# Chunk attention and a leaky two-layer product on one core: a build-time order that lets a load on Pool wait for the landing of the eighth preceding one, with 14 instead of 16 pieces by seven products

## The chip, the core and the metric

The kernel runs on one core of a Trainium2 chip. The core has a matrix engine (PE), a vector engine (DVE), a scalar engine (ACT), Pool (GpSimd) and SP, which here only issues transfers. Each engine works through its own list of instructions in order and waits on semaphores for the others. The metric is the time of one execution on the device in microseconds. A profiled execution gives the trace that the views are made from; its span runs from the first to the last instruction of the program.

## The reference

Inputs are q, k and v of shape (8 batches, 8 heads, 576, 64) and the weights w_in (512 x 2048) and w_out (2048 x 512), all float32.

```python
# attention inside chunks of 64 positions, nc = 9 chunks
scores = (1 / np.sqrt(D)) * np.matmul(q_c, k_c.transpose(0, 1, 2, 4, 3))
scores = scores - np.max(scores, axis=-1, keepdims=True)
attn = np.exp(scores)
attn = attn / (np.sum(attn, axis=-1, keepdims=True) + 1e-09)
out = np.matmul(attn, v_c)
...
# x: (4608 tokens, 512), heads side by side
h = x @ w_in
g = np.maximum(0.01 * h, h)
return (g @ w_out).astype(np.float32)
```

## The kernel before

**Attention by groups.** The 4608 tokens are 36 groups of 128 (two chunks, all eight heads). For a group `u`: its q and k are loaded by Pool's queue and cast to fp16 (`q_in`, `k_in`, eight buffers each, `NIN`); transposed; multiplied to scores (`Sp`, PE, L412); row maxima are taken and subtracted (`mx`, `sh`, DVE); ACT takes the exponential (`ex`); DVE sums and inverts (`z`, `ze`, `zi`); the result is normalised (`en`, on DVE, from group 24 on Pool); transposed again (`et`); multiplied by v (`xp`, PE, L477) and copied by ACT into the ring `xT`, where the second stage reads it. From group 9 on the transposes are DMA transposes issued by SP (`QT`, `KT`, `et`), and Pool copies the transposed q into the two zero-padded halves of a `QZ` buffer (L405, two copies per group, three buffers). The eight batches of v go into two buffers `VB`; batch b + 2 is loaded, in two halves, when the last `xp` that reads batch b has run.

**Two layers by blocks.** The tokens are also cut into 14 blocks, from block 7 on of 512 tokens. The first layer (w_in, then the leaky ReLU on ACT into `gT`) of a block runs beside the second layer of the block before. A block's first layer has four quarters. From block 8 on a plain quarter is four pieces of eight matmuls of 256 columns (`hT`, L165, 32 matmuls), each evicted by one ACT operation. A quarter can also be formed by seven products of half size in place of eight (`first_fast`, L763): 28 matmuls of 256 columns (`hA`, `hB`, `hC`, L297), three ACT copies to `tmp`, three DVE additions (L220), four leaky ReLUs on ACT. It needs four sums of weights (`VF`, formed once) and, per block, four differences of the inputs (`XF`, `x_form`, L257, on DVE). `FAST` says how many quarters of a block are formed so. The second layer of blocks 7 to 13 is always done by seven products (`second_fast`, L813), with sums of `gT` formed on DVE (`g_form`, L308).

**What sets the order.** Up to the middle of block 2 the order is written out by hand, loads included. After that a planner that runs while the program is built sets it. Each unit of work is a `Step` with an engine, an assumed duration, the steps it comes after, a key and a latency until others may use its result; `run()` (L574) repeatedly takes, over all engines, the step that can begin first (among those within 0.03 us on one engine the one with the smallest key), advances that engine's clock and emits the step's instructions. The plan moves nothing at run time: it decides in which order instructions stand in each engine's list. PSUM banks and `tmp` buffers are taken and given back by steps, so the plan also decides who shares a buffer.

In the plan a load was two steps: `load` on Pool (0.86 us, or 1.7 in two parts), then `arrive` on a separate timeline "dma" (2.05 us each, one after another, latency 2.5). Transposes on SP were given a latency of 10 us.

In the built program every DMA that Pool issues signals one of eight semaphores in turn. From the ninth on, a load waits at the head of Pool's list for the semaphore of the eighth preceding one. That wait stands in the program before as well as in the changed one.

Of the kernel before, what the change touches and what calls it, by code (L numbers as in the profile page):

```python
# [16 lines left out]
def kernel(  # L17
# [11 lines left out]
    B, H, S, D = q.shape  # L29
# [10 lines left out]
    NIN = 8  # L40
    UD = 9
    G = 2 * CH
# [5 lines left out]
    RING = 1536  # L48
    HB, HM = NFC // 2, d_model // 2
    NTMP = 7  # L50
    FAST = {10: 4, 11: 4, 12: 4, 13: 4}
    POOL_N, POOL_X = 24, 20

    sbp = ctx.enter_context(tc.tile_pool(name="k_sb", bufs=1))
# [519 lines left out]
    def run():  # L574
        now = {e: 0.0 for e in LAT}
        now["pool"] = 10.0
        left = {id(s): len(s.after) for s in steps}
        users: dict[int, list[Step]] = {}
        for s in steps:
            for x in s.after:  # L580
                users.setdefault(id(x), []).append(s)
        can = {e: [] for e in LAT}
        for s in steps:
            if not s.after:
                can[s.eng].append(s)
        INF = float("inf")

        def begin(s):
            t = max([now[s.eng], s.at] + [x.end + (x.lat if x.eng != s.eng or x.lat > 1 else LAG[s.eng]) for x in s.after])
            for pool in {h.pool for h in s.take}:  # L590
                n = sum(h.pool == pool for h in s.take)
                slots = sorted(y[0] for y in free[pool])
                if len(slots) < n + s.spare:
                    return INF
                t = max(t, slots[n - 1])
            return t

        order = []
        n = 0
        while True:  # L600
            best = None
            for e in LAT:
                if not can[e]:
                    continue
                at = [(begin(s), s) for s in can[e]]
                t0 = min(x[0] for x in at)
                if t0 == INF:
                    continue
                t, s = min((x for x in at if x[0] <= t0 + 0.03), key=lambda x: x[1].key)
# [24 lines left out]
    LAG = {"pe": 0.0, "act": 0.1, "dve": 0.1, "pool": 0.0, "sp": 0.0, "dma": 0.0}  # L634
    Step.spare = 0
    Step.name = ""

    def add(name, *a, spare=0, **k):
# [6 lines left out]
    get = done.get  # L645
# [6 lines left out]
    def group(u):  # L652
        at = max(0.0, BEGIN + (u - 5) * PACE)
        k = u / 4
        dve, act = 10 + k, 10 + k
        for i in range(2):
            if u >= UD + 4:
                add(("load", u, i), "pool", 0.86 if (u * G) // S == (u * G + G - 1) // S else 1.7, lambda u=u, i=i: load_half(u, i),
                    [get(("t", u - NIN, i)) or get(("pe_t", u - NIN, i)), get(("arrive", u - 4, i))], key=5 + u / 100, lat=0.5)
                add(("arrive", u, i), "dma", 2.05, lambda: None, [get(("load", u, i))], key=u, lat=2.5)  # L660
            elif u > 5:
                add(("arrive", u, i), "dma", 0.9, lambda: None, [], key=-9, at=2.2 + 1.8 * (u - 6) + 0.9 * i, lat=2.0)
        if 5 < u < UD:
            for i in range(2):
                h = Hold("bank")
                add(("pe_t", u, i), "pe", 0.23, lambda u=u, i=i, h=h: (stage_tq, stage_tk)[i](u, h.slot), [get(("arrive", u, i))],
                    key=-3, take=[h], spare=1)
                if i == 0:
                    for s in range(2):
                        add(("p", u, s), "dve", 0.42, lambda u=u, s=s: stage_q(u, s), [get(("pe_t", u, 0)), get(("s", u - NQZ))],  # L670
                            key=dve, give=[h] if s else [])
                else:
                    add(("k", u), "act", 0.5, lambda u=u: stage_k(u), [get(("pe_t", u, 1)), get(("s", u - 4))], key=act, give=[h])
        elif u >= UD:
            for i in range(2):
                add(("t", u, i), "sp", 1.28, lambda u=u, i=i: stage_t(u, i),
                    [get(("arrive", u, i)), get(("p", u - 4, 1)), get(("s", u - 4))], key=u, lat=10.0)
            for s in range(2):
                add(("p", u, s), "pool", 0.67, lambda u=u, s=s: stage_p(u, s), [get(("t", u, 0)), get(("s", u - NQZ))], key=u / 100)
        if u >= 5:  # L680
            h = Hold("bank")
            need = [get(("p", u, 0)), get(("p", u, 1)), get(("k", u)) or get(("t", u, 1))]
            add(("s", u), "pe", 0.24, lambda u=u, h=h: stage_s(u, h.slot), need, key=-2, take=[h], at=at)
            add(("m", u), "dve", 0.61, lambda u=u: stage_m(u), [get(("s", u)), get(("b", u - 2))], key=dve - 6)
            add(("b", u), "dve", 0.61, lambda u=u: stage_b(u), [get(("m", u)), get(("x", u - 2))], key=dve - 6, give=[h])
            add(("x", u), "act", 0.52, lambda u=u: stage_x(u), [get(("b", u)), get(("n", u - 2))], key=act - 4)
            add(("z", u), "dve", 1.15, lambda u=u: stage_z(u), [get(("x", u)), get(("n", u - 2))], key=dve - 4)
            add(("n", u), "pool" if u >= POOL_N else "dve", 1.0 if u >= POOL_N else 0.61, lambda u=u: stage_n(u),
                [get(("z", u)), get(("d", u - 3)) or get(("e", u - 3))], key=-1 if u >= POOL_N else dve - 4)
        if u < UD:  # L690
            h = Hold("bank")
            add(("e", u), "pe", 0.23, lambda u=u, h=h: stage_e(u, h.slot), [get(("n", u))], key=-2, take=[h])
            add(("d2", u), "dve", 0.34, lambda u=u: stage_c(u), [get(("e", u)), get(("v", u - 4))], key=dve - 3, give=[h])
        else:
            add(("d", u), "sp", 1.28, lambda u=u: stage_d(u), [get(("n", u)), get(("v", u - 4))], key=u, lat=10.0)
# [117 lines left out]
    def second_fast(j, k0):  # L813
        key = ("o", j)
        g = lambda f, e: G_OF[j, f, e]
        f0 = add(("sf", j, 0), "dve", 1.14, lambda: g_form(j, 0), g(0, 1) + g(1, 1) + [get(("m2", j - 1, 5, p)) for p in range(2)], key=6 + k0)
        f1 = add(("sf", j, 1), "dve", 1.14, lambda: g_form(j, 1), [f0] + g(0, 0) + [get(("m2", j - 1, 6, p)) for p in range(2)], key=6 + k0)
        f2 = add(("sf", j, 2), "dve", 1.14, lambda: g_form(j, 2), [f0] + g(0, 0), key=7 + k0)
# [56 lines left out]
        f3 = add(("sf", j, 3), "dve", 1.14, lambda: g_form(j, 3), [f1] + p2, key=6.5 + k0)  # L875
# [60 lines left out]
    for j in range(4, len(BLOCKS)):  # L936
# [10 lines left out]
        if fast:  # L947
            x = [y for y in x_of(j, 0, 512)]
            for i in range(4):
                add(("xf", j, i), "pool" if j >= POOL_X else "dve", 1.0 if j >= POOL_X else 0.35, lambda j=j, i=i: x_form(j, i),  # L950
                    x + ([get(("xf", j, {1: 0, 3: 1}[i]))] if i in (1, 3) else [])
                    + [get(("f", jj, ii, {0: 5, 1: 6, 2: 7, 3: 4}[i])) for jj, ii in fast_n if jj == j - 1],
                    key=5.8 + place)
# [46 lines left out]
```

## Time and profile before

| | us |
|---|---|
| median of three runs | 288.58 |
| lowest, highest | 287.51, 289.36 |
| the profiled execution's own time | 289.68 |
| span in its trace | 287.9 |
| mean granted clock of PE (share of full) | 0.988 |

What Pool's loads take from issue to landing, and SP's transposes, stands in the page's list of DMA issues (size, median us to landing):

```profile
q_in<-in_q_dram POOLq DMA_DIRECT2D x31, 128.0 KB, 7.1
k_in<-in_k_dram POOLq DMA_DIRECT2D x31, 128.0 KB, 7.5
...
QT<-q_in SPq DMA_TRANSPOSE x27, 6.2
KT<-k_in SPq DMA_TRANSPOSE x27, 5.9
et<-en SPq DMA_TRANSPOSE x27, 5.4
```

Rows of the other views are read like this. In groups of instructions: line, engine, operation, tile written, tile read, shapes, count, then busy us, mean ns of one, and the idle time of the engine just before them with what ended it. In the timeline: start, duration, instruction, and in brackets the idle time before it. Who ended an idle time is inferred from semaphores; where the engine named had long been done, another did. In the slices each digit is a fortieth of the span in tenths.

### The profile page before, as it was taken

The page shows a single profiled execution, that of the slowest core. Times are in us where ns is not written, and L with a number is a line of the kernel's source. Part 1 is how long each engine was busy: PE and PEld are TensorE (multiplying, and loading weights), DVE is VectorE, ACT ScalarE, POOL GpSimd, SP SyncE. Part 2 cuts the span into 40 slices and gives each one's busy share as a digit, 9 for nine tenths or more (in the row PEclk, how much of TensorE's full clock was granted, in tenths as well). Part 3 has the DMA queues.
Part 4 walks back from the last instruction along what each step waited for, and adds up shares of the span by engine and source line. Part 5 has one row for each costly group of instructions (what it writes and reads, how often), then busy time and mean ns, then how long its engine had stood idle before and what let it go on. Part 6 is the DMA issues. An engine that isn't in the chain of part 4 may idle for free.

```text
span 287.9 us, 7650 instructions
## 1 busy us (share of the span) xinstructions
PE 270.9 (94%) x3124; PEld 232.1 (81%) x3124; DVE 212.2 (74%) x364; ACT 176.1 (61%) x319; POOL 143.6 (50%) x178
## 2 busy tenths in 40 slices
PE   4989999994999999999999999988998999999995
PEld 4979846863686899999898988877797898988884
DVE  6988415993598569886966499988988994685472
ACT  6357723751464773737665449972699689578721
POOL 8857557937498256952985287674641111000000
PEclk9999999998699999999999999999999999999999
DMA  9999999999999999999999999997952101300223
GB/s 131 164 191 193 205 158 198 160 144 150 155 151 156 155 175 143 168 136 243 144 124 149 193 181 148 93 194 147 154 139 77 34 3 36 148 2 0 87 98 109
DMA packets 165794, 39.16 MB, mean 136 GB/s; under 512 B 156800, under 2 KB 161408, under 8 KB 165760
## 3 DMA queue, kind: packets, MB, share of 16 engines
q0 software_dynamic: 114336, 18.09, 94.8%
q1 hardware_dynamic: 50384, 20.33, 39.0%
q8 instruction: 24, 0.39, 0.6%
q10 hardware_dynamic: 1040, 0.26, 0.4%
q14 instruction: 10, 0.08, 0.1%
HBM read 36.70 MB, written 9.44 MB: 160 GB/s over the span
## 4 chain that ended last, share of the span: by engine, by line
PE 73%; DVE 14%; ACT 4%; issue 3%; POOL 3%; DMA 2%; DVEq 0%; ACTq 0%; POOLq 0%
PE hT L165 22%; PE oA L342 13%; PE oP L190 10%; PE hA L297 7%; PE oC L342 6%; PE hC L297 3%; PE oB L342 3%; PE Sp L412 2%; PE xp L477 2%; DVE tmp L220 2%; PE hB L297 2%; DMA k_f<-in_k_dram 2%; DVE gT L217 2%; DVE z L437 2%; DVE mx L421 2%
## 5 line engine op out<-in xcount | busy, mean ns | idle before, releaser
L165 PE MATMUL hT<-xT,w_inT 128*128 128x128 f16 (+1 forms) x960 | 79.3, 239 | 0.2 <-issue 0.2
L165 PEld LDWEIGHTS <-w_inT 128*128 128x128 f16 x960 | 68.0, 99 | 6.9 <-issue 0.9
L175 ACT ACTIVATE gT<-hT 128x512 f16<-128x512 f32 x80 | 47.3, 595 | 35.4 <-PE hT L165 34.9
L342 PEld LDWEIGHTS <-gT 128*128 128x128 f16 x560 | 54.1, 98 | 7.4 <-issue 1.3
L405 POOL COPY QZ<-QT 64x512 f16<-64x512 f16 x54 | 39.5, 732 | 16.1 <-DMA QT<-q_in 13.8
L421 DVE TENSOR_REDUCE mx<-Sp 128x8 f32<-128x512 f32 x36 | 24.5, 681 | 12.8 <-PE Sp L412 12.6
L175 ACT ACTIVATE gT<-tmp 128x512 f16<-128x512 f32 x48 | 29.7, 632 | 5.3 <-DVE tmp L220 5.3
L437 DVE TENSOR_REDUCE z<-ex 128x8 f32<-128x512 f16 x36 | 24.4, 679 | 11.3 <-ACT ex L431 11.2
L178 ACT ACTIVATE tmp<-hA 128x512 f32<-128x512 f32 x48 | 27.6, 598 | 7.9 <-PE hA L297 7.9
L190 PE MATMUL oP<-w_outT,gT 128*128 128x512 f16 x128 | 31.6, 387 | 0.0
L220 DVE TENSOR_TENSOR tmp<-hC,tmp 128x512 f32<-128x512 f32 x32 | 21.7, 681 | 11.3 <-ACT tmp L178 7.2
L489 ACT ACTIVATE xT<-xp 128x512 f16<-128x512 f32 x36 | 21.3, 594 | 14.0 <-PE xp L477 13.8
L431 ACT ACTIVATE ex<-sh 128x512 f16<-128x512 f32 x36 | 22.7, 630 | 10.8 <-DVE sh L425 10.1
L342 PE MATMUL oA<-WF,gT 128*128 128x256 f16 x224 | 27.9, 272 | 1.0 <-ACT tmp L178 1.0
L297 PEld LDWEIGHTS <-VF 128*128 128x128 f16 x256 | 24.6, 98 | 4.0 <-DVE XF L262 0.7
L447 POOL TENSOR_TENSOR en<-ex,zi 128x512 f16<-128x512 f16 x12 | 12.5, 1042 | 30.1 <-DVE zi L441 23.7
L912 POOL DMA_DIRECT2D VB<-in_v_dram x12 | 13.9, 1158 | 25.0 <-PE xp L477 25.0
L425 DVE TENSOR_TENSOR sh<-Sp,mx 128x512 f32<-128x512 f32 x36 | 24.5, 681 | 0.5
L342 PEld LDWEIGHTS <-S 128*128 128x128 f16 x224 | 20.9, 98 | 4.9 <-DVE S L220 2.2
L905 POOL DMA_DIRECT2D k_in<-in_k_dram x26 | 22.1, 853 | 4.1 <-PE hT L165 3.7
L905 POOL DMA_DIRECT2D q_in<-in_q_dram x26 | 22.1, 854 | 3.5 <-PE tpe L455 2.9
L178 ACT ACTIVATE tmp<-oA 128x512 f32<-128x512 f32 (+1 forms) x24 | 13.0, 540 | 15.7 <-PE oA L342 15.7
(71 smaller groups left out, 453.9 us busy)
## 6 DMA issues: line engine op xcount, KB each, us to landing
out_dram<-osb SPq DMA_DIRECT2D x12, 512.0 KB, 3.6
VB<-in_v_dram POOLq DMA_DIRECT2D x16, 288.0 KB, 7.3
q_in<-in_q_dram POOLq DMA_DIRECT2D x31, 128.0 KB, 7.1
k_in<-in_k_dram POOLq DMA_DIRECT2D x31, 128.0 KB, 7.5
out_dram<-osb SPq DMA_DIRECT2D x10, 256.0 KB, 5.5
w_inT<-in_moe_w_in_dram POOLq DMA_DIRECT2D x8, 256.0 KB, 8.8
w_outT<-in_moe_w_out_dram POOLq DMA_DIRECT2D x4, 512.0 KB, 10.3
q_in<-in_q_dram POOLq DMA_DIRECT2D x8, 64.0 KB, 9.4
```

The costliest lines, as they stand in the source:

```text
L165: nc.tensor.matmul(out=hT[:, i, :], lhsT=w_inT[:, t, fc * 128:(fc + 1) * 128], rhs=xT[:, t, r0 % RING:r0 % RING + tb], start=(t == 0), sto ...
L175: nc.scalar.activation(out=to, in_=of, func=AFT.Prelu, bias=0.0, scale=1.0, alpha=0.01)
L178: nc.scalar.activation(out=to, in_=of, func=AFT.Copy, bias=0.0, scale=1.0)
L190: nc.tensor.matmul(out=OP[j, ti], lhsT=gT(j)[:, fc, ti * 128:(ti + 1) * 128], rhs=w_outT[:, fc, :], start=(fc == 0), stop=(fc == NFC - 1),)
L220: nc.vector.tensor_tensor(out=to, in0=a, in1=b, op=ALU.add)
L297: nc.tensor.matmul(out=PA[key][:, c, :], lhsT=w[:, t, fc * 128:(fc + 1) * 128], rhs=x[:, t, :], start=(m in OPENS and c == 0 and t == 0), ...
L342: nc.tensor.matmul(out=to, lhsT=lhs[:, fc, p * 128:(p + 1) * 128], rhs=rhs[:, fc, :], start=(fresh and fc == 0), stop=(fc == HB - 1), skip ...
L405: nc.gpsimd.tensor_copy(out=QZ[u % NQZ][part, :, :, s, :], in_=QT[u][part])
L421: nc.vector.tensor_reduce(out=MX[u], in_=SP[u], axis=AXL.X, op=ALU.max)
L425: nc.vector.tensor_tensor(out=SH[u], in0=SP.pop(u), in1=MX.pop(u).unsqueeze(2).to_broadcast((128, 8, CH)), op=ALU.subtract)
L437: nc.vector.tensor_reduce(out=z, in_=E[u], axis=AXL.X, op=ALU.add)
L905: nc.gpsimd.dma_start(out=t[a - r0:z - r0], in_=src[a // S, :, a % S:a % S + z - a, :].rearrange("h p d -> p h d"),)
```

## The change

The plan is told of the eight semaphores. A list `landed` holds the planned landing times of Pool's loads; a step with loads cannot begin before the landing of the eighth preceding one, and its own landing is the later of the last landing plus a duration (2.0 us for a load, 1.0 for a part, 4.4 for half of v) and 4.0 us after its end. `load` and `arrive` become one step on Pool whose latency is set when it is placed. Loads keep their order among themselves through `follow`. A transpose that begins after the last landing in the plan has a latency of 4.5 instead of 10. Some assumed durations change: the normalisation on Pool 1.05 (1.0), the sums of `gT` 1.2 (1.14), the `XF` forms 0.5 (0.35). `FAST` becomes 1, 2, 3, 4, 4 quarters in blocks 9 to 13 instead of 4 in each of blocks 10 to 13.

```diff
-    FAST = {10: 4, 11: 4, 12: 4, 13: 4}
+    FAST = {9: 1, 10: 2, 11: 3, 12: 4, 13: 4}
...
         def begin(s):
-            t = max([now[s.eng], s.at] + [x.end + (x.lat if x.eng != s.eng or x.lat > 1 else LAG[s.eng]) for x in s.after])
+            t = max([now[s.eng], s.at] + ([landed[len(s.dmas) - 9]] if s.dmas else []) + [x.end + (0 if x is s.follow else x.lat if x.eng != s.eng or x.lat > 1 else LAG[s.eng]) for x in s.after])
...
+        landed = [LANDED + 0.9 * (i - 7) for i in range(8)]
...
             s.begin, s.end = t, t + s.us
+            for us in s.dmas:
+                landed.append(max(landed[-1] + us, s.end + LATE))
+                s.lat = landed[-1] - s.end
+            if s.eng == "sp" and s.lat == TURNED and landed[-1] < t:
+                s.lat = QUIET
...
+    TURNED, QUIET, LATE, LANDED = 10.0, 4.5, 4.0, 16.2
...
-                add(("load", u, i), "pool", 0.86 if (u * G) // S == (u * G + G - 1) // S else 1.7, lambda u=u, i=i: load_half(u, i),
-                    [get(("t", u - NIN, i)) or get(("pe_t", u - NIN, i)), get(("arrive", u - 4, i))], key=5 + u / 100, lat=0.5)
-                add(("arrive", u, i), "dma", 2.05, lambda: None, [get(("load", u, i))], key=u, lat=2.5)
+                whole = (u * G) // S == (u * G + G - 1) // S
+                x = add(("arrive", u, i), "pool", 0.86 if whole else 1.7, lambda u=u, i=i: load_half(u, i),
+                        [get(("t", u - NIN, i)) or get(("pe_t", u - NIN, i))], key=5 + u / 100)
+                x.dmas = [2.0] if whole else [1.0, 1.0]
+                x.follow = get(("arrive", u, 0) if i else ("arrive", u - 1, 1)) if i or u > UD + 4 else None
+                x.after += [x.follow] if x.follow else []
...
-                    add(("load_v", b2 + 2, m), "pool", 1.14, lambda b=b2 + 2, m=m: load_v_half(b, m), [get(("v", u))], key=4, lat=0.5)
-                    last = add(("v_in", b2 + 2) if m else ("v_in0", b2 + 2), "dma", 4.4, lambda: None, [get(("load_v", b2 + 2, m))], key=b2 * 4.5)
+                    x = add(("v_in", b2 + 2) if m else ("v_in0", b2 + 2), "pool", 1.14, lambda b=b2 + 2, m=m: load_v_half(b, m), [get(("v", u))], key=4)
+                    x.dmas = [4.4]
```

In the built program this moves instructions within each engine's list. Pool's first difference is after the load of group 15's q: the four `QZ` copies of groups 9 and 10 now stand ahead of three loads they stood behind. PE's list is the same until the first `xp` of group 9, DVE's and ACT's until about the same place. PE has 960 + 64 matmuls of `hT` in place of 960 (two of these quarters, 64) and 56 fewer of the seven products; DVE has two instructions fewer, ACT six.

More of the change, by code (lines that the diff above doesn't have):

```diff
@@ L632, in run @@
         return order
+    TURNED, QUIET, LATE, LANDED = 10.0, 4.5, 4.0, 16.2
     LAG = {"pe": 0.0, "act": 0.1, "dve": 0.1, "pool": 0.0, "sp": 0.0, "dma": 0.0}
     Step.spare = 0
+    Step.dmas = ()
+    Step.follow = None
     Step.name = ""
@@ L676, in group @@
                 add(("t", u, i), "sp", 1.28, lambda u=u, i=i: stage_t(u, i),
-                    [get(("arrive", u, i)), get(("p", u - 4, 1)), get(("s", u - 4))], key=u, lat=10.0)
+                    [get(("arrive", u, i)), get(("p", u - 4, 1)), get(("s", u - 4))], key=u, lat=TURNED)
             for s in range(2):
@@ L687, in group @@
             add(("z", u), "dve", 1.15, lambda u=u: stage_z(u), [get(("x", u)), get(("n", u - 2))], key=dve - 4)
-            add(("n", u), "pool" if u >= POOL_N else "dve", 1.0 if u >= POOL_N else 0.61, lambda u=u: stage_n(u),
+            add(("n", u), "pool" if u >= POOL_N else "dve", 1.05 if u >= POOL_N else 0.61, lambda u=u: stage_n(u),
                 [get(("z", u)), get(("d", u - 3)) or get(("e", u - 3))], key=-1 if u >= POOL_N else dve - 4)
@@ L694, in group @@
         else:
-            add(("d", u), "sp", 1.28, lambda u=u: stage_d(u), [get(("n", u)), get(("v", u - 4))], key=u, lat=10.0)
+            add(("d", u), "sp", 1.28, lambda u=u: stage_d(u), [get(("n", u)), get(("v", u - 4))], key=u, lat=TURNED)
         h = Hold("bank")
@@ L815, in second_fast @@
         g = lambda f, e: G_OF[j, f, e]
-        f0 = add(("sf", j, 0), "dve", 1.14, lambda: g_form(j, 0), g(0, 1) + g(1, 1) + [get(("m2", j - 1, 5, p)) for p in range(2)], key=6 + k0)
-        f1 = add(("sf", j, 1), "dve", 1.14, lambda: g_form(j, 1), [f0] + g(0, 0) + [get(("m2", j - 1, 6, p)) for p in range(2)], key=6 + k0)
-        f2 = add(("sf", j, 2), "dve", 1.14, lambda: g_form(j, 2), [f0] + g(0, 0), key=7 + k0)
+        f0 = add(("sf", j, 0), "dve", 1.2, lambda: g_form(j, 0), g(0, 1) + g(1, 1) + [get(("m2", j - 1, 5, p)) for p in range(2)], key=6 + k0)
+        f1 = add(("sf", j, 1), "dve", 1.2, lambda: g_form(j, 1), [f0] + g(0, 0) + [get(("m2", j - 1, 6, p)) for p in range(2)], key=6 + k0)
+        f2 = add(("sf", j, 2), "dve", 1.2, lambda: g_form(j, 2), [f0] + g(0, 0), key=7 + k0)
         wf = [get(("wf", q)) for q in range(4)]
@@ L874, in second_fast @@
         s11 = sum_of("d", 0, lo, [x + osb_free() for x in two(p2, d)], B1)
-        f3 = add(("sf", j, 3), "dve", 1.14, lambda: g_form(j, 3), [f1] + p2, key=6.5 + k0)
+        f3 = add(("sf", j, 3), "dve", 1.2, lambda: g_form(j, 3), [f1] + p2, key=6.5 + k0)
         p6 = mm(6, [[y, f1, wf[1]] for y in (d if last else d * 2)])
@@ L949 @@
             for i in range(4):
-                add(("xf", j, i), "pool" if j >= POOL_X else "dve", 1.0 if j >= POOL_X else 0.35, lambda j=j, i=i: x_form(j, i),
+                add(("xf", j, i), "pool" if j >= POOL_X else "dve", 1.6 if j >= POOL_X else 0.5, lambda j=j, i=i: x_form(j, i),
                     x + ([get(("xf", j, {1: 0, 3: 1}[i]))] if i in (1, 3) else [])
```

## The prediction

> **What bounds the kernel now.** I read the page's busy shares first, then its slices.
>
> ```profile
> span 287.9 us, 7650 instructions
> PE 270.9 (94%) x3124; PEld 232.1 (81%) x3124; DVE 212.2 (74%) x364; ACT 176.1 (61%) x319; POOL 143.6 (50%) x178
> ...
> PE   4989999994999999999999999988998999999995
> ...
> PEclk9999999998699999999999999999999999999999
> ```
>
> PE is busy 94% of the span, so only its idle or slowed time can be won. The slices say where that is: the two ends, the tenth slice (65 to 72 us, PE 4, then clock 8 and 6), and a shallow dip from about 190 us. PE's waits (total, times, longest) say for whom:
>
> ```profile
> PE Sp L412 <- POOL QZ L405: 4.0, 2, 3.8
> ...
> PE oC L342 <- DVE S L220: 1.6, 1, 1.6
> PE oA L342 <- ACT tmp L178: 1.0, 2, 0.7
> PE hA L297 <- ACT tmp L178: 1.0, 1, 1.0
> ...
> PE hA L297 <- DVE XF L262: 0.4, 1, 0.4
> ```
>
> The first is almost wholly one wait of 3.8 us: the scores of group 9 for Pool's copies into QZ. The chain of waits shows it and what follows (start, us, what):
>
> ```profile
> 69.30 0.64 POOL QZ L405
> ...
> 70.65 0.61 PE Sp L412 x8
> 71.26 1.71 PE hT L165 x8
> ...
> 77.76 0.87 PE hT L165 x8
> ```
>
> Eight first-layer matmuls take 1.71 us just after the wait and 0.87 us later. Three stretches of the windows view say why (busy PE, PEld, DVE, ACT, POOL, then granted clock):
>
> ```profile
> 60.00:66.80 6.80, 6.80 (x64) 4.19 (x62) 6.73 (x11) 2.83 (x5) 1.34 (x2) 1.00 1.81 126
> ...
> 70.65:76.65 6.00, 6.00 (x38) 3.87 (x39) 4.24 (x8) 1.71 (x3) 2.44 (x4) 0.52 2.17 152
> 78.00:138.00 60.00, 60.00 (x759) 52.26 (x758) 46.48 (x77) 36.11 (x64) 38.69 (x48) 1.00 1.91 161
> ```
>
> The clock is 1.00 before the wait and 0.52 for 6.0 us behind it. So the one wait costs 3.8 us idle and 6.00 x (1 - 0.52) = 2.9 us of slow work, 6.7 us together; afterwards PE runs 60 us without a gap.
>
> **Part one, the load queue.** Pool's timeline, with the idle time before an instruction in brackets, then how long the loads of V issued at 51.4 and 52.6 us took to land, and the same for the Q transposes of groups 9 and 10 (issued at 53.80 and 56.68 us) and the K transpose of group 9 (55.26 us):
>
> ```profile
> 61.79 0.87 POOL L905 DMA_DIRECT2D q_in<-in_q_dram  x1 [2.90 <-PE tpe L455]
> 66.33 0.88 POOL L905 DMA_DIRECT2D k_in<-in_k_dram  x1 [3.67 <-PE hT L165]
> ...
> 69.30 3.97 POOL L405 COPY QZ<-QT 64x512 f16<-64x512 f16 x6
> ```
>
> ```profile
> DMA to landing us min/median/max: 9.8/11.5/13.2
> ```
>
> ```profile
> 53.80 1.35 SPq L399 DMA_TRANSPOSE QT<-q_in  x1
> 55.26 1.37 SPq L399 DMA_TRANSPOSE KT<-k_in  x1
> 56.68 1.44 SPq L399 DMA_TRANSPOSE QT<-q_in  x1
> ```
>
> ```profile
> DMA to landing us min/median/max: 9.1/9.2/9.2
> ```
>
> ```profile
> DMA to landing us min/median/max: 9.4/9.4/9.4
> ```
>
> The brackets blame PE, which had long been done. The V halves landed at 51.4 + 9.8 = 61.2 and 52.6 + 13.2 = 65.8 us, each half a microsecond before the load that stands eight loads later: the wait for the eighth preceding landing is real in the kernel before too. The old plan did not know it, so it put four loads ahead of the QZ copies of group 9, whose Q had landed at 53.80 + 9.1 = 62.9 us. They ran at 69.30.
>
> In the changed order Pool's list is the same up to the load that runs at 61.79; then come both copies of group 9, both of group 10, and only then the load that waited until 66.33. PE's list is the same until after the scores of group 12, and DVE's and ACT's are still the same there, so times can be carried over. Group 9's copies start at 62.9 and, at 1.3 us a pair, end at 64.2; its K lands at 55.26 + 9.4 = 64.7. PE reaches these scores at 66.9 (70.65 less 3.8). The wait goes, with 2.2 us to spare, and the slow clock with it: **-6.7 us**.
>
> The clock's part can be read two ways. The Trainium skill, TensorE: Matmul & The Clock Gate, Part 1: The HAM clock gate, has the array fall to half speed after an idle window of about 3.4 us and return after about 3.4 us of sustained work; by that the slow work would cost an estimated 1.7 us and this part 5.5. The trace has 6.0 us at 0.52, so the trace's 2.9 stands.
>
> What is late next? Group 10's scores come 5 us of matmuls later (71.9); its Q landed at 56.68 + 9.2 = 65.9, copied by 67.3. The loads now behind these copies are issued about 1 us later than before and feed groups 15 and 16, whose scores lie 30 us on. Farther on, the loads of V wait at the head of Pool's line for PE's last use of a buffer, and what stands behind them waits too:
>
> ```profile
> L912 POOL DMA_DIRECT2D VB<-in_v_dram x12 | 13.9, 1158 | 25.0 <-PE xp L477 25.0
> ```
>
> In the changed order the worst such place has two V loads (2.3 us), a normalisation (1.0), five loads (at most 0.87 each, 4.4) and a copy pair (1.3) before the scores of group 28: 9.0 us, with 13.5 us of matmuls to cover them. At the others it is 6.3 us or less under 10 or more.
>
> **Part two, 14 pieces.** A piece by seven products is 7 x 4 = 28 matmuls of 256 columns; the plain quarter it stands for is 32. Two fewer pieces add 8 matmuls, one row of 0.87 us: **+0.9 us**, all on PE, with no cover.
>
> The pieces also move: 4, 4, 4, 4 in blocks 10 to 13 become 1, 2, 3, 4, 4 in blocks 9 to 13. What a piece asks of the other engines (busy us, mean ns):
>
> ```profile
> L220 DVE TENSOR_TENSOR tmp<-hC,tmp 128x512 f32<-128x512 f32 x32 | 21.7, 681 | 11.3 <-ACT tmp L178 7.2 <-PE hC L297 4.0
> ...
> L262 DVE TENSOR_TENSOR XF<-xT 128x512 f16<-128x512 f16 x8 | 4.8, 637 | 0.0
> L262 DVE TENSOR_TENSOR XF<-xT,XF 128x512 f16<-128x512 f16 x8 | 3.7, 464 | 0.0
> ```
>
> ```profile
> L175 ACT ACTIVATE gT<-hT 128x512 f16<-128x512 f32 x80 | 47.3, 595 | 35.4 <-PE hT L165 34.9
> L175 ACT ACTIVATE gT<-tmp 128x512 f16<-128x512 f32 x48 | 29.7, 632 | 5.3 <-DVE tmp L220 5.3
> L178 ACT ACTIVATE tmp<-hA 128x512 f32<-128x512 f32 x48 | 27.6, 598 | 7.9 <-PE hA L297 7.9
> ```
>
> DVE: 3 additions of 0.68 = 2.0 us. ACT: 7 operations of about 0.61 = 4.3 us, against 4 of 0.595 = 2.4 for the plain quarter, so 1.9 more. Blocks 10 and 11 lose three pieces: 6.1 us of DVE and 5.7 of ACT leave the stretch after 170 us, where the seven-product work now begins. Block 9 gains one piece and four XF forms, 2.0 + 2 x 0.64 + 2 x 0.46 = 4.2 us of DVE, ahead of that. The two stretches:
>
> ```profile
> 160.00:170.00 10.00, 10.00 (x124) 9.07 (x122) 7.99 (x10) 4.59 (x8) 3.95 (x4) 1.00 1.34 214
> 170.00:230.00 60.00, 55.86 (x605) 48.72 (x603) 55.26 (x101) 45.74 (x88) 30.80 (x39) 1.00 1.12 123
> ```
>
> After 170 us DVE is busy 55.26 of 60 and PE idles 60 - 55.86 = 4.1; all four late waits above, 4.0 us, are for results of DVE or ACT. With 6.1 us taken out DVE falls from 92% to 82%. The changed order shows the relief in one more way: between the row maximum and the reciprocal of groups 24 to 28 DVE had 18, 19, 21, 23, 16 instructions in line and now has 6, 6, 14, 9, 6. How much of 4.0 comes back is between 0 and 4.0; a queue that loses more than half of its surplus should lose more than half of its waits, so I take two thirds: **-2.7 us**. Against it, a new order brings new short waits that no row shows. They lie between 0 and the longest late wait, 1.6 us; below zero is excluded, since I already credit the waits that go. I take **+0.7**. The changed durations and landing times in the plan cost nothing by themselves: they emit no instruction.
>
> **Sum.** -6.7 + 0.9 - 2.7 + 0.7 = -7.8 us, against the profiled execution's own 289.68 us (span 287.9 and 1.8 around it): 281.9. That run was 1.1 above the median of 288.58, so the median goes to **280.8 us**.
>
> **Rivals.** *The first wait goes, the late ones stay* (chance 0.20): DVE's queue is as long in the second layer's forms as before, or the earlier pieces move the crowd instead of thinning it. -6.7 + 0.9, with up to 3 us of new waits: 283 to 285.7. For it: DVE was at 8 of 10 us even before 170, where work is added. Against: the totals fall.
>
> *The wait moves* (0.13): Pool's copies come in time but another landing does not, since loads and transposes share the engines (transposes took 9 us there against 3 to 6 later), and PE idles long enough elsewhere for the clock to fall again. One such repeat is worth the same 6.7: -7.8 + 6.7 = -1.1, 287.5; 285.7 to 291.5 with the rest open. That the edit does nothing, because the waits on landings stand in the kernel before already, ends here too; the order speaks against it.
>
> *Slower* (0.07): Pool's normalisation stands ahead of QZ copies. In the changed order one half of group 29's copy is behind the normalisation of group 27. The times before:
>
> ```profile
> 171.09 0.41 PE L412 MATMUL Sp<-KT,QZ 128*128 128x64 f16 x8
> ...
> 183.97 1.03 POOL L447 TENSOR_TENSOR en<-ex,zi 128x512 f16<-128x512 f16 x1 [2.12 <-DVE zi L441]
> ```
>
> These are the scores and the normalisation of group 26, 13.9 us from the start of one to the end of the other. Scores 27 and 29 are 10.9 us of matmuls apart in the new order; if the path stays 13.9 and half a copy pair, 0.6, follows it, PE waits 3.6 us and the clock falls, 6.5 us. Groups 30 and 32 stand the same way: 11.6 us apart, path and a whole pair 15.2, again 3.6 and 6.5. With a path that long the late waits do not come back either: -6.7 + 0.9 + 0.7 + 13.0 = +7.9, 296.5. It decides from a path longer than 10.3 us at both places. Against: 9 instructions stand in DVE's line instead of 23. The Trainium skill, SBUF — State Buffer, SBUF: two separate sides, adds that a Pool operation and a DVE operation with two SBUF inputs lock each other out; no row here separates that from other causes of a long copy.
>
> **Numbers.** Forecast case 0.60, from 278.2 (all 4.0 us back, no new waits, half a microsecond of scatter) to 283. With the first rival 0.80 and a little of the second, 278.2 to 286.5 holds 8 in 10; about 0.05 lies below, 0.15 above. A measurement here can tell about 1% from no change, 2.9 us: faster than 285.7 has 0.80, within 1% 0.13, slower 0.07.
>
> **What would show it.** Right: PE's wait for QZ at the scores of group 9 is gone, granted clock 1.00 from 66 to 78 us, QZ copies starting near 63 us; PE idle after 170 us near 2 us, DVE busy there under 52 of 60; 1024 matmuls of hT instead of 960 and 56 fewer of the seven products. Wrong: any PE wait over 3 us after 20 us with a clock below 1.00 behind it, normalisations on Pool over 10 us after their scores, or late PE idle still at 4 us.

## The result, and the profile after

| us | before | after |
|---|---|---|
| median (four runs each, taken together) | 288.54 | 284.69 |
| lowest, highest | 287.51, 289.36 | 283.20, 285.20 |
| the profiled execution's own time, span | 289.68, 287.9 | 284.97, 283.2 |
| mean granted clock of that execution | 0.988 | 1.000 |

The changed kernel takes 0.986 of the time before, with a 95% interval of 0.981 to 0.991: about 4 us faster, where 7.8 were forecast. Medians are over all runs; ratios leave out the slow ones, more than 1.5% above the fastest of the same kernel. The page after, its shares and slices:

```profile
span 283.2 us, 7648 instructions
PE 268.6 (95%) x3132; PEld 231.7 (82%) x3132; DVE 211.3 (75%) x362; ACT 173.6 (61%) x313; POOL 140.7 (50%) x178
...
PE   4989999999999999989899998999789999999995
...
PEclk9999999999999999999999999999999999999999
```

The 4 in PE's tenth slice and the 8 and 6 in the clock are gone. Two stretches of the windows view (busy PE, PEld, DVE, ACT, POOL, granted clock) and the timeline of Pool and of PE around group 9 say the same more sharply:

```profile
66.80:78.00 11.20, 11.20 (x150) 9.37 (x149) 10.53 (x18) 7.50 (x15) 9.94 (x13) 1.00 1.72 166
...
170.00:230.00 60.00, 56.77 (x627) 50.08 (x625) 51.02 (x87) 41.90 (x79) 27.42 (x34) 1.00 1.26 136
```

```profile
63.52 2.21 POOL L405 COPY QZ<-QT 64x512 f16<-64x512 f16 x2 [2.37 <-DVE sh L425]
...
67.15 0.40 PE L412 MATMUL Sp<-KT,QZ 128*128 128x64 f16 x8
```

The copies for group 9 begin at 63.52 and its scores run at 67.15 with no bracket behind them, so without a wait, and PE has no gap from 66.8 to 78 us. But PE's waits now bear other names than before:

```profile
PE xp L477 <- DMA et<-en: 5.0, 5, 1.3
...
PE Sp L412 <- DMA KT<-k_in: 0.7, 1, 0.7
```

Not one late wait for a result of DVE or ACT is left (4.0 us of them before). In their place PE waits five times for a DMA transpose of `en` and once for one of k, together 5.7 us, none longer than 1.3. The chain of waits names the same stage, with shares of the span:

```profile
PE 77%; DMA 12%; DVE 6%; SPq 2%; issue 1%; ACT 1%; DVEq 0%; ACTq 0%
PE hT L165 21%; PE oA L342 15%; DMA et<-en 10%; PE oP L190 10%; PE hA L297 8%; PE oC L342 7%; PE hC L297 4%; PE oB L342 3%; PE xp L477 3%; PE Sp L412 2%; PE hB L297 2%; SPq L399 2%; DMA k_f<-in_k_dram 2%; DVE z L437 1%; DVE S L220 1%
```

How late these transposes land, and the loads with them, is in the list of DMA issues (count, KB each, median us from issue to landing):

```profile
q_in<-in_q_dram POOLq DMA_DIRECT2D x31, 128.0 KB, 15.2
k_in<-in_k_dram POOLq DMA_DIRECT2D x31, 128.0 KB, 15.5
...
QT<-q_in SPq DMA_TRANSPOSE x27, 8.5
KT<-k_in SPq DMA_TRANSPOSE x27, 8.1
et<-en SPq DMA_TRANSPOSE x27, 8.4
```

A load took 7 us before and takes 15 now; a transpose took 5.4 to 6.2 and takes 8.1 to 8.5. The bytes are the same. Pool's groups say what is different, in the idle time before each load and what ended it:

```profile
L917 POOL DMA_DIRECT2D q_in<-in_q_dram x26 | 21.9, 842 | 13.9 <-DMA k_in<-in_k_dram 4.2 <-DMA q_in<-in_q_dram 4.1 <-DMA VB<-in_v_dram 3.3
L917 POOL DMA_DIRECT2D k_in<-in_k_dram x26 | 21.7, 836 | 13.3 <-DMA k_in<-in_k_dram 5.8 <-DMA VB<-in_v_dram 2.1 <-DMA q_in<-in_q_dram 2.1
L924 POOL DMA_DIRECT2D VB<-in_v_dram x12 | 13.9, 1158 | 4.5 <-DMA q_in<-in_q_dram 3.0 <-PE hT L165 1.0 <-DMA k_in<-in_k_dram 0.4
```

Before, the loads of V stood 25.0 us at the head of Pool's list for PE, and every load behind them stood too. I read that as a brake on the loads too. Now V waits 4.5 us, and it is the loads of q and k that wait, for the landing of the eighth preceding one: as soon as one lands the next goes out, and up to eight are under way. Counted in the two traces, 2 of Pool's transfers (median) stood between issue and landing when an `et` was issued before, and 7 after; from 78 to 190 us it is 3.0 and 7.5 on average. The transposes run beside that traffic, and SP, which issues them, falls behind as well:

```profile
191.35 1.05 POOL L447 TENSOR_TENSOR en<-ex,zi 128x512 f16<-128x512 f16 x1 [0.44 <-ACT gT L175]
...
192.15 2.76 SPq L466 DMA_TRANSPOSE et<-en  x1
195.00 1.78 SPq L399 DMA_TRANSPOSE QT<-q_in  x1
196.88 1.56 SPq L399 DMA_TRANSPOSE KT<-k_in  x1
198.53 2.16 SPq L399 DMA_TRANSPOSE QT<-q_in  x1
200.80 1.21 SPq L466 DMA_TRANSPOSE et<-en  x1
...
208.57 0.41 PE L477 MATMUL xp<-et,VB 128*128 128x64 f16 x8 [0.78 <-DMA et<-en]
```

This is group 30: `en` was done at 192.40, its transpose was issued at 200.80, behind four others, landed 7.7 us later, and PE waited 0.78 us for it. Over the 27 groups, `en` waited 15.7 us for SP before and 51.4 us after (sum of the gaps from the end of `en` to the start of its transpose on SP).

**The account.** Between the two profiled executions 4.7 us went. PE's busy time fell by 2.3 (2.9 of slow clock, less 0.9 for the pieces, and 0.3 that I did not trace); its idle time after 20 us (gaps over 0.1 us, here and below) fell from 8.4 to 6.2; 0.2 lies ahead of that.

### The profile page after: what moved, and what is told of

Same layout as the page of the kernel before. It is cut to its first block, busy times and chain, and to the rows that moved or that the text cites. A ratio compares the mean times of both kernels' runs of the same rounds, so it can differ in the third digit from the quotient of the medians.

```text
span 283.2 us, 7648 instructions
## 1 busy us (share of the span) xinstructions
PE 268.6 (95%) x3132; PEld 231.7 (82%) x3132; DVE 211.3 (75%) x362; ACT 173.6 (61%) x313; POOL 140.7 (50%) x178
## 4 chain that ended last, share of the span: by engine, by line
PE 77%; DMA 12%; DVE 6%; SPq 2%; issue 1%; ACT 1%; DVEq 0%; ACTq 0%
PE hT L165 21%; PE oA L342 15%; DMA et<-en 10%; PE oP L190 10%; PE hA L297 8%; PE oC L342 7%; PE hC L297 4%; PE oB L342 3%; PE xp L477 3%; PE Sp L412 2%; PE hB L297 2%; SPq L399 2%; DMA k_f<-in_k_dram 2%; DVE z L437 1%; DVE S L220 1%
## 5 line engine op out<-in xcount | busy, mean ns | idle before, releaser
L165 PE MATMUL hT<-xT,w_inT 128*128 128x128 f16 (+1 forms) x1024 | 85.7, 239 | 0.8 <-issue 0.5
L165 PEld LDWEIGHTS <-w_inT 128*128 128x128 f16 x1024 | 73.1, 98 | 6.9 <-issue 1.3
L175 ACT ACTIVATE gT<-hT 128x512 f16<-128x512 f32 x88 | 51.9, 595 | 30.6 <-PE hT L165 30.2
L342 PEld LDWEIGHTS <-gT 128*128 128x128 f16 x560 | 54.2, 98 | 6.2
L405 POOL COPY QZ<-QT 64x512 f16<-64x512 f16 x54 | 36.6, 678 | 24.6 <-DMA QT<-q_in 16.8
L175 ACT ACTIVATE gT<-tmp 128x512 f16<-128x512 f32 x42 | 26.1, 630 | 8.9 <-DVE tmp L220 8.9
L178 ACT ACTIVATE tmp<-hA 128x512 f32<-128x512 f32 x42 | 24.6, 596 | 10.2 <-PE hA L297 10.1
L190 PE MATMUL oP<-w_outT,gT 128*128 128x512 f16 x128 | 30.6, 380 | 0.0
L220 DVE TENSOR_TENSOR tmp<-hC,tmp 128x512 f32<-128x512 f32 x28 | 19.1, 686 | 14.2 <-ACT tmp L178 7.7
L431 ACT ACTIVATE ex<-sh 128x512 f16<-128x512 f32 x36 | 22.6, 628 | 11.5 <-DVE sh L425 11.2
L917 POOL DMA_DIRECT2D q_in<-in_q_dram x26 | 21.9, 842 | 13.9 <-DMA k_in<-in_k_dram 4.2
L297 PEld LDWEIGHTS <-VF 128*128 128x128 f16 x224 | 21.5, 98 | 2.4
L190 PEld LDWEIGHTS <-gT 128*128 128x128 f16 x128 | 11.7, 98 | 10.9
## 6 DMA issues: line engine op xcount, KB each, us to landing
q_in<-in_q_dram POOLq DMA_DIRECT2D x31, 128.0 KB, 15.2
```

The lines of the kernel that those rows point to most:

```text
L165: nc.tensor.matmul(out=hT[:, i, :], lhsT=w_inT[:, t, fc * 128:(fc + 1) * 128], rhs=xT[:, t, r0 % RING:r0 % RING + tb], start=(t == 0), sto ...
L175: nc.scalar.activation(out=to, in_=of, func=AFT.Prelu, bias=0.0, scale=1.0, alpha=0.01)
L178: nc.scalar.activation(out=to, in_=of, func=AFT.Copy, bias=0.0, scale=1.0)
L190: nc.tensor.matmul(out=OP[j, ti], lhsT=gT(j)[:, fc, ti * 128:(ti + 1) * 128], rhs=w_outT[:, fc, :], start=(fc == 0), stop=(fc == NFC - 1),)
L297: nc.tensor.matmul(out=PA[key][:, c, :], lhsT=w[:, t, fc * 128:(fc + 1) * 128], rhs=x[:, t, :], start=(m in OPENS and c == 0 and t == 0), ...
L342: nc.tensor.matmul(out=to, lhsT=lhs[:, fc, p * 128:(p + 1) * 128], rhs=rhs[:, fc, :], start=(fresh and fc == 0), stop=(fc == HB - 1), skip ...
```

## The experiments

The kernel before ran beside all of them. In 17 of these 59 runs its mean clock was 0.998 or more (median 286.3 us), in 32 it was 0.992 to 0.994 (288.5), in 10 it was 0.987 or 0.988 (290.5). So what the clock costs varies from run to run; the profile shown ahead of the prediction is of the kind that loses most, and of the other runs of that kernel no trace is kept, so that a shorter wait in them is not excluded. Ratios are against the runs of the kernel before that were taken along with the experiment; waits, landings and idle times are those of one profiled execution of each kernel.

**Each part alone.** The first kernel has the new order with the old pieces, the second the old order with the new pieces.

```diff
-    FAST = {9: 1, 10: 2, 11: 3, 12: 4, 13: 4}
+    FAST = {10: 4, 11: 4, 12: 4, 13: 4}
```

> The new plan with the old 16 pieces (4 in each of blocks 10 to 13). If the thinner and earlier pieces are what took away the late waits for DVE and ACT (theory A), they come back here: 2 to 4 us of PE waits for results of DVE or ACT after 170 us, and 285 to 287.5 us although PE has 0.9 us less to do. If the order of the new plan alone did it (rival), none come back and the time is 283.8, the changed kernel's 284.7 less 0.9. Both theories: no wait of PE for QZ at group 9, clock 1.00.

```diff
-    FAST = {10: 4, 11: 4, 12: 4, 13: 4}
+    FAST = {9: 1, 10: 2, 11: 3, 12: 4, 13: 4}
```

> The old plan with the new 14 pieces. Theory A: the wait of 3.8 us at the scores of group 9 and 6 us of half clock stay, the late waits for DVE and ACT (4.0 us) mostly go, 0.9 us of matmuls come: 288.5 + 0.9 - 3 = 286.4, between 285.4 and 288. Rival (the pieces thin nothing out): 289 to 290. Transposes as quick as in the kernel before, median 5.4 to 6.2 us, because the loads are not pulled forward.

Measured: the order alone 286.71 us, ratio 0.995 [0.990, 1.000]; the pieces alone 287.33, ratio 0.999 [0.995, 1.004]. The waits of PE and the windows of the first:

```profile
PE oC L342 <- DVE S L220: 2.8, 1, 2.8
```

```profile
193.00:199.00 6.00, 6.00 (x52) 4.88 (x53) 5.43 (x8) 1.63 (x3) 2.25 (x3) 0.72 1.28 183
```

With the old pieces the first wait goes, but a wait for DVE of 2.8 us is left where the pieces crowd, and the clock falls to 0.72 behind it; eight of its ten runs have a mean clock of 0.994 or less. Waits for `et`, 2.6 us in all, are there too. That is what theory A forecast for this kernel. With the new pieces and the old order the first wait stays (timeline and windows of the second kernel):

```profile
69.48 0.41 PE L412 MATMUL Sp<-KT,QZ 128*128 128x64 f16 x8 [2.07 <-POOL QZ L405]
```

```profile
70.00:78.00 8.00, 8.00 (x94) 6.43 (x93) 7.39 (x12) 5.49 (x10) 6.57 (x10) 1.00 2.08 185
```

In this execution it was 2.07 us and the clock did not fall; the other nine runs have a mean clock of 0.994 or 0.988, so it fell in them, where is not known. Of the late waits for DVE and ACT 2.2 us of 4.0 stayed, so the pieces alone thin less than theory A had it; its range held, but by the ratio 0.2 us were won and not 2.1, which cannot be told from nothing. `et` landed in 6.6 us, later than the 5.4 to 6.2 expected. The gains of the parts by the ratios, 1.5 and 0.2 us, do not add up to the 4 of both: each leaves a place where PE stands for two or three microseconds, and it took both parts to clear both.

**Why PE waits for `et`: late issue or late landing.** Two theories. One (B): SP puts transposes of q and k ahead of `et`, so it is issued late. The other (C): the transposes land late since eight loads share their engines. The first kernel puts q's and k's transposes of group u behind `et` of group u - 4 in SP's list:

```diff
-                add(("t", u, i), "sp", 1.28, lambda u=u, i=i: stage_t(u, i),
-                    [get(("arrive", u, i)), get(("p", u - 4, 1)), get(("s", u - 4))], key=u, lat=TURNED)
+                x = add(("t", u, i), "sp", 1.28, lambda u=u, i=i: stage_t(u, i),
+                        [get(("arrive", u, i)), get(("p", u - 4, 1)), get(("s", u - 4))], key=u, lat=TURNED)
+                x.follow = get(("d", u - 4))
+                x.after += [x.follow] if x.follow else []
```

> The changed kernel, but the q and k transposes of group u stand behind the transpose of the normalised scores (et) of group u - 4 in SP's list. In the changed kernel PE waits 5.0 us in five places for et. Theory B (et is issued late, behind transposes that are needed later): the time from the normalisation's end to et's issue falls from 2 to 8 us to under 2, the waits fall by half or more, 282 to 283.5 us. Theory C (et lands late, 8 to 10 us after its issue, because loads and transposes share the engines): landing stays above 8 us, the waits fall by less than 1.5 us, 283.8 to 285.5.

The second has the changed kernel's order, with the loads of q of groups 17 to 35 left out: these groups read group 16's q.

```diff
     def load_half(u, i):
+        if i == 0 and u > 16:
+            qk[u] = (qk[16][0], None)
+            return
```

> The changed kernel in the same order, but the q loads of groups 17 to 35 are left out (these groups read group 16's q), so that half of the load traffic after 75 us is gone. Theory C: et lands in under 6 us (8.4 before), PE's waits for et after 120 us go, near 281 us. Theory B: SP issues et as late as before, the waits stay within 1 us of what they were, 284 us.

Measured: `et` first 284.46 us, ratio 0.991 [0.987, 0.994], no better than the change. The gaps between `en` and SP fell from 51.4 to 26.0 us, but the idle time of PE stayed (6.2 us after 20 us); it moved to one `xp` and to four scores. The waits for `et` fell by about half, as theory B had it, and `et` landed in 7.0 us, sooner than theory C asked for, but the time is in C's range: neither forecast held whole (waits of PE):

```profile
PE xp L477 <- DMA et<-en: 2.7, 1, 2.7
PE Sp L412 <- POOL QZ L405: 1.6, 4, 0.7
```

Without the q loads, one run: 280.38 us, span 278.6. Its wait for `et` (at 95 us, none after 120) and its DMA issues:

```profile
PE xp L477 <- DMA et<-en: 1.6, 1, 1.6
```

```profile
k_in<-in_k_dram POOLq DMA_DIRECT2D x31, 128.0 KB, 7.9
q_in<-in_q_dram POOLq DMA_DIRECT2D x14, 128.0 KB, 8.8
QT<-q_in SPq DMA_TRANSPOSE x27, 6.4
KT<-k_in SPq DMA_TRANSPOSE x27, 6.6
et<-en SPq DMA_TRANSPOSE x27, 5.2
```

With half of the loads of q and k from group 17 on gone, `et` lands in 5.2 us, SP's backlog is gone too (13.8 us), and PE's idle time after 20 us is 2.0 instead of 6.2 us: 4.3 of the 4.6 us that the span is shorter. So the loads cause both the late landing and the late issue, and in these runs mending the issue alone does not pay.

**The first wait alone.** In the kernel before, only the load of group 15's k is put behind the `QZ` copies of groups 9 and 10. The lists of PE, DVE, ACT and SP stay as they were.

```diff
-                    [..., get(("arrive", u - 4, i))], key=5 + u / 100, lat=0.5)
+                    [..., get(("arrive", u - 4, i)), get(("p", 10, 1)) if (u, i) == (15, 1) else None], key=5 + u / 100, lat=0.5)
```

> The kernel before with one added order: the load of group 15's k stands behind the QZ copies of groups 9 and 10. PE's, DVE's, ACT's and SP's lists are the kernel before's to the last instruction; Pool's differs in a few places around these copies. It prices the first wait alone. If the first wait was worth its 3.8 us and the 2.9 us of half clock in every run: 6.7 us less, 281 to 282. If the clock falls only in some runs (it did not in the profile of the pieces-only kernel, whose wait was 2.1 us): 2 to 5 us less, 283 to 286. If the time is given back to later waits for et, as in the changed kernel: 285 to 288, with et landing later than 5.4 us.

Measured: 288.21 us, ratio 0.996 [0.992, 1.000]. The wait at group 9 went, and the scores of group 20 ran at 129.81 in place of 133.55 us, 3.7 us earlier. The first wait itself was worth more: this execution was behind at its start (1.3 us of waiting for a landing of w_in, then 3.4 us at half clock), so that group 8's scores ran 2.1 us later than before (62.73 against 60.59), and group 10's ran 4.1 us earlier (74.34 against 78.47). That is 6.3 us won between the two, near the 6.7 forecast. At group 21 nearly all that was left was lost again (Pool's timeline, then PE's, then the windows):

```profile
131.01 2.31 POOL L912 DMA_DIRECT2D VB<-in_v_dram  x2 [3.89 <-PE xp L477]
134.68 0.88 POOL L905 DMA_DIRECT2D q_in<-in_q_dram  x1 [1.37 <-DMA q_in<-in_q_dram]
138.82 0.88 POOL L905 DMA_DIRECT2D k_in<-in_k_dram  x1 [3.25 <-DMA k_in<-in_k_dram]
139.74 1.28 POOL L405 COPY QZ<-QT 64x512 f16<-64x512 f16 x2
```

```profile
141.07 0.41 PE L412 MATMUL Sp<-KT,QZ 128*128 128x64 f16 x8 [3.41 <-POOL QZ L405]
```

```profile
141.10:148.00 6.90, 6.90 (x66) 5.69 (x67) 3.09 (x4) 2.90 (x6) 6.09 (x8) 0.75 1.97 152
```

The scores of group 21 run at 141.07, where they had run at 141.64 before: loads that wait for a landing stand ahead of that group's copies too, and that had been hidden behind the first wait. So none of the three forecasts held: `et` did land later (7.2 us, loads of q 11.5), but PE waited only 0.2 us for it, and the time went to the next copies instead. Mending this place as well (the copies of group 21 ahead of the loads of V's batch 5 and of group 27):

```diff
-                    [..., get(("p", 10, 1)) if (u, i) == (15, 1) else None], ...)
+                    [..., get(("p", 10, 1)) if (u, i) == (15, 1) else get(("p", 21, 1)) if u == 27 else None], ...)
...
-                    add(("load_v", b2 + 2, m), ..., [get(("v", u))], key=4, lat=0.5)
+                    add(("load_v", b2 + 2, m), ..., [get(("v", u)), get(("p", 21, 1)) if b2 + 2 == 5 else None], key=4, lat=0.5)
```

> The kernel before with group 9's wait mended as in the run before of this kind, and also with group 21's QZ copies put ahead of the loads of batch 5's v and of group 27. In that run PE reached the scores of group 21 earlier, waited 3.4 us there for QZ behind those loads, and ended no sooner. Theory D (Pool's line is paced by landings all along, so a wait that is mended passes to the next place): PE's wait at group 21 goes, another of 1 us or more comes after it (QZ or et), and 285 to 287.5 us remain. Rival (two bad places, and with both mended the time is won): 281.5 to 284, no wait over 1 us between 20 and 190 us.

Measured: 285.28 us, ratio 0.990 [0.984, 0.996]. In its profiled run (288.06 us) the wait at group 21 was gone, but group 9 waited 2.9 us again:

```profile
66.47 0.88 POOL L905 DMA_DIRECT2D q_in<-in_q_dram  x1 [5.17 <-DMA VB<-in_v_dram]
```

A load of q had slipped ahead of the copies and stood 5.2 us for a landing. The other three runs took 284.8 to 285.7. This pair is not a clean test of either reading: two places mended by hand are worth 2.9 us by the ratio (4.0 by the medians), but Pool's list shifts a little and the first wait can come back.

**Fewer loads under way.** In the changed kernel a load of group u is put behind the `QZ` copies of group u - 3, u - 4 or u - 5 (here 4), which limits how far loads run ahead:

```diff
                 x.after += [x.follow] if x.follow else []
+                x.after.append(get(("p", u - 4, 1)))
```

> The changed kernel, but in the plan a load of group u comes after the QZ copies of group u - 3, so it stands later in Pool's list; the same loads, fewer in flight. Theory C1 (depth: transposes share the engines with up to eight loads that wait in the queue): loads land in 7 to 9 us instead of 15, et in under 7 instead of 8.4, PE's waits for et fall below 2 us in all, 281.5 to 283. Theory C2 (volume: the engines have no room whatever the order): et stays at 8 us or more, or PE waits for the later loads instead, 284 to 287.

> As the run before, with the QZ copies of group u - 4: about one group earlier. Theory C1: between the changed kernel and the run before, et landing 7 to 8 us, 282.5 to 284. Theory C2: 284 to 285.

> The changed kernel with a load of group u behind the QZ copies of group u - 5, one group earlier than in the run with u - 4, which gave 283.49 against 284.52 of the changed kernel on the same chip, with et landing in 5.7 us instead of 8.1. Theory C1: more loads in flight, et 6.5 to 8 us, PE's waits for et 0 to 3 us, 283 to 284.5. If it is not the depth: no order among the three, et at 5.7.

The changed kernel itself and the version with four were run again. The first version with four was taken together with u - 3 and the change, the second together with u - 5:

> The changed kernel once more on the same chip, so that the other runs of this call can be compared with it: 284 to 285.5, et landing 8.4 us, PE's waits for et 3 to 6 us.

> Loads behind the QZ copies of group u - 4 once more, to be compared with the others of this call: 283 to 284, et landing 5.5 to 6.5 us, no wait of PE for et over 0.5 us.

| loads behind group | us, median | ratio, interval | under way | `et` lands in | q and k land in | PE idle after 20 us |
|---|---|---|---|---|---|---|
| u - 3 | 302.79 | 1.050 [1.045, 1.055] | 1 | 4.1 | 5.4, 6.8 | 18.2 |
| u - 4 | 283.49 | 0.984 [0.978, 0.990] | 3 | 5.7 | 8.0, 8.3 | 5.7 |
| u - 4, again | 283.36 | 0.982 [0.977, 0.986] | 2 | 4.9 | 7.3, 7.9 | 4.4 |
| u - 5 | 283.26 | 0.980 [0.975, 0.986] | 6 | 7.7 | 12.0, 12.7 | 3.6 |
| the change, again | 284.52 | 0.988 [0.983, 0.993] | 7 | 8.1 | 14.5, 13.2 | 6.8 |

"Under way" is the median number of Pool's transfers between issue and landing when an `et` is issued. Pool's groups and one row of the DMA issues of the second run with u - 4:

```profile
L918 POOL DMA_DIRECT2D k_in<-in_k_dram x26 | 22.0, 851 | 0.0
L918 POOL DMA_DIRECT2D q_in<-in_q_dram x26 | 22.0, 847 | 0.0
```

```profile
et<-en SPq DMA_TRANSPOSE x27, 4.9
```

No load of q or k waits any longer, the transposes land as in the kernel before, and PE has no wait for `et`. Its longest waits after 20 us are these:

```profile
PE oC L342 <- DVE S L220: 2.4, 2, 1.7
PE hT L165 <- ACT xT L489: 0.9, 1, 0.9
```

So the cause of the waits for `et` is removed, and yet the time gains only some 1.1 us on the change: the plan sets another order, and waits for DVE and ACT come back. These are the shortest median times measured with the whole computation, but the intervals of the change and of u - 4 overlap, so that the last microsecond isn't certain. The waits themselves differ between executions of one kernel: the change, again, waited 2.8 us for `et` and 1.7 for `QZ`, where it had been 5.0 and none. With u - 3 the transposes land soonest, and as I read it the loads come too late: PE's 18 us of idle time are spread over `xp` (3.9), scores (2.2) and many waits for DVE and ACT. With u - 5 the landings are nearly as late as in the change, yet PE waits only 0.7 us for `et`; the median landing alone does not decide, and what does there stays open.

**Truer durations in the plan.** The version with u - 4, with the measured durations of DVE's and ACT's attention steps and evictions in place of the plan's (0.68 for 0.61 on DVE, 0.60 to 0.62 for 0.50 to 0.52 on ACT):

```diff
-            add(("m", u), "dve", 0.61, ...)
+            add(("m", u), "dve", 0.68, ...)
...
-        add(("a", u), "act", 0.5, ...)
+        add(("a", u), "act", 0.6, ...)
```

> Loads behind the QZ copies of group u - 4, and the plan's durations of ACT and DVE set to those that the trace shows (0.68 instead of 0.61 for a DVE operation of 512 columns, 0.6 to 0.62 instead of 0.5 to 0.52 on ACT). Theory E: with the loads out of the way the waits that are left (for S, for tmp, for xT, 5 us in the run with u - 4) come from a plan that takes DVE and ACT for 10 to 20% faster than they are; they fall by half, 281 to 282.5. Rival: they come from the pieces themselves and the order they allow; 283 to 285.

Measured: 288.59 us, ratio 1.000 [0.996, 1.004]: 5 us worse than without, above both forecasts, and 287.4 in the seven runs with a full clock. PE's waits, and the window behind the wait of 2.4 us (clock 0.51):

```profile
PE oC L342 <- DVE S L220: 3.3, 3, 2.2
PE hT L165 <- ACT xT L489: 3.1, 2, 2.4
```

```profile
129.40:132.90 3.50, 3.50 (x17) 2.50 (x17) 1.35 (x4) 0.60 (x1) 2.17 (x3) 0.51 1.21 160
```

Here truer durations gave a worse order, with longer waits of the same kind. Why stays open.

## Why the prediction came out as it did

**The wait at group 9 (-6.7).** Right in its mechanism and nearly to the figure: copies at 63.5 for a forecast of 62.9, scores at 67.15 for 66.9, no wait, clock 1.00; and 6.3 us were won at this place when its wait alone was taken out. As a price for the median, 6.7 was too high. It took the clock's part, 2.9 us, from one execution, which was among the slowest-clocked of the kernel. The median run of the kernel before has a clock of 0.992 to 0.994, and by the medians such a run is 2.2 us above one with a full clock. The traces show why there are three levels. Before, the clock was at half for 6.8 us:

```profile
69.40:76.30 6.90, 5.65 (x31) 3.60 (x32) 3.89 (x8) 1.71 (x3) 3.57 (x6) 0.51 2.13 158
```

That is 6.9 x (1 - 0.51) = 3.4 us of clock, 2.9 of it on work and the rest while PE still waited. The other falls shown above lose half as much: 6.0 x (1 - 0.72), 6.9 x (1 - 0.75) and 3.5 x (1 - 0.51) are 1.7 us each. In 288 us, 1.7 is a clock of 0.994 and 3.4 one of 0.988, so by their mean clocks 17 of the 59 runs have no such stretch, 32 have one and 10 have two. The Trainium skill, TensorE: Matmul & The Clock Gate, Part 1: The HAM clock gate, says that the activity window of 3.4 us is free-running and that the start of the same kernel therefore varies from run to run; the traces agree for waits in mid-kernel (a wait of 2.41 us was followed by a fall, one of 2.71 was not). The 0.5 us that the medians show beyond 1.7 stays open. So the 1.7 us which the prediction set aside is closer to most runs than the row it took.

**Two fewer pieces (+0.9).** Right in the count: 1024 matmuls of `hT`, 8 more matmuls on PE. Their price was not measured apart.

**The late waits (-2.7 of 4.0).** Right in kind and too small: all 4.0 went. DVE is busy 51.0 of the 60 us after 170, under the 52 named. The idle time of that stretch is 3.2 us and not the 2 forecast, but none of it is DVE's or ACT's any more. The order alone left 2.8 us of such waits and the pieces alone 2.2, so this needs both.

**New short waits (+0.7, at most 1.6).** This is the step that failed, a term of the sum that was too small: they came to 5.7 us. They were taken as one short wait of DVE or ACT, bounded by the longest late one; they are six waits for landings. The second rival, in which another landing is late because loads and transposes share the engines, named the mechanism, but asked for one long wait and a fall of the clock: 1.3 us was the longest, and the clock stayed full. The prediction followed the `QZ` copies past every load and asked whether q and k come in time; it never followed `et`, which goes through SP's list and the same engines. And it read the 25 us that V's loads stood on Pool as a nuisance to the copies behind them, and did not ask whether they kept the number of loads under way small.

**The sum.** From 280.8: 0.7 for the clock's part (2.2 in place of 2.9), 5.0 more for new waits and 1.3 less for the late ones make 285.2; 284.7 was measured. The forecast was 3.9 us too low, inside its range. It is outside the forecast case (278.2 to 283) and in the band of the first rival (283 to 285.7), whose reason, late waits that stay, did not come true. That the time still fell into the range is in part luck: the late waits gave more than forecast, and that hid a part of the new ones.

**The rivals.** That the late waits stay did not happen. "Slower" did not either: the path it feared was shorter, since the normalisation of group 27 ended 8.4 us after its scores, where 13.9 had been taken over from group 26, and `QZ` for group 29 was ready 2.8 us early. The sign set for it was a poor one: five groups from the 26th on did take over 10 us from their scores to the end of the normalisation (the longest 14.3), and no scores waited for a copy.

## What to carry to other kernels

A plan that lets transfers start earlier has changed every transfer that shares their engines: follow each of those to its reader, not only the one that was late. A wait that ends may have been a brake, so count how many transfers are under way before and after, and try a limit below the program's own. Price a fall of the clock over several runs, and expect the next wait in the same list to take back what one mended place gives, as group 21 did.

## What the runs showed of the hardware

- A DMA transpose's time to landing goes with the loads under way: medians of 4.1, 4.9, 7.7 and 8.4 us where loads of q took 5.4, 7.3, 12.0 and 15.2, with the same bytes in all four. Counted within the trace of the kernel before, a transpose (median) landed in 2.6 us with none of Pool's transfers beside it, in 4.2 with about one, 5.3 with two, 7.2 with four, and 8.0 to 9.2 with more. Some transfer of Pool was under way for 95% of the time from 78 to 190 us before and for all of it after, so it is not the mere presence of one that changed. The Trainium skill, DMA: Bandwidth & Descriptors, Queues, rings and completion order, has each engine go round between the queues that have work, packet by packet; that fits a transpose slowed by any load beside it, but not by itself one that more loads slow further. More transposes are under way at those times too, and the runs do not part the two.
- To issue a transpose held SP for 1.2 us when it went well, for 2.76 us in the row of group 29 and for 3.7 us once in the kernel with `et` first. All 81 transposes together held it for 112 us before, 129 after, and 112 with u - 3; single long ones are in all three (2.7, 3.2 and 2.9 us).
- Each fall of the clock behind a wait in mid-kernel lasted 3.4 us, or twice that, at half clock (six in the kept traces). The length of the wait alone does not decide: waits of 2.07, 2.54 and 2.71 us passed without a fall, waits of 2.41, 2.81, 2.86 and 3.41 us cost one such stretch, and 3.78 and 3.94 us cost two.
